# Half of the next v joined between a step's choice of experts and its counts; halves of the sums of squares added before the reduction

## Chip, cores, metric

One NeuronCore of a Trainium2 chip runs the whole program in one launch. The metric is the device time of the execution in microseconds, as the median of several runs. Single stretches come from a profile of one execution, in which every instruction has its engine, its start and its duration.

## What is computed

The first half is an attention over channels, the second a mixture of experts with one expert for each token:

```
B, N, C = 4, 5056, 256          T = B*N = 20224 tokens, E = 8, F = 1024
qn = q / (norm(q, over N) + 1e-6);  kn likewise            # norms of columns
s  = kn^T @ qn / tau                                        # C x C per batch
a  = softmax(s);   x = v @ a                                # N x C per batch
logits = x @ w_gate + modality_bias[modality_id]
e  = argmax(logits);  gate = softmax(logits)[e]
out[token] = gate * (relu(x @ w1[e]) @ w2[e])
```

All inputs are f32. The kernel splits each f32 factor of a large product in a rounded high part and a low remainder and adds three products (high by high, high by low, low by high).

## The kernel before, in words

The tokens of a batch come in NS = 10 steps of 512 (the last has 448), 40 steps g in all. Three kinds of work run beside each other.

- **q and k** (`kq_pieces`): for each step, q and k are loaded (`load`), split (`split`, lines 312 and 313), multiplied into the sum `g` in PSUM (`mm`, line 357), and squared (line 336). DVE adds the squares to `acc` (line 338), which has two halves of 2 x 256 columns, for q and for k. They are made one batch ahead.
- **softmax of a batch** (`softmax_pieces`): `norms` turns `acc` into inverse norms, by matmuls with a matrix of ones (lines 379 and 384); then `soft` per half and `gate_weights` give the attention matrix, extended by the columns of its product with w_gate.
- **a step of v** (`va_pieces`): `fetch` brings v transposed, as 16-bit halves, to the tile `T` by a transposing DMA; `part` (four DMAs in `halves`, line 506) sorts the halves into the tile `pl`; `tr(h)`, h = 0 and 1, joins them to f32 in a tile `vt` (lines 512 on ScalarE, 513 on VectorE) and splits it into `vh` and `vl` (lines 560 and 561); `av(t)`, t = 0 to 3, multiplies with the attention matrix (line 574: six matmuls into `xp`), and copies out x (lines 580, 581) and the logits `L` (line 582). `route` (lines 588 to 614) makes the one-hot choice `oh` of the experts and the running count `run` of each token's expert, and the parts of the gate. `place` (lines 625 to 647) has three small bf16 matmuls `rp`, which read `oh` and `run` and count over the partitions; from them come the rows of the tokens, and at the end `send` scatters x to its rows in the DRAM tile `xs` from GpSimd's queue. Tiles `vh` and `vl` have two buffers, `pl` and `T` one each.
- **a block of 512 rows of one expert** (`block_pieces`): from step `first_block` = 6 on one block runs per step; `load_x` and `load_w` load its rows and weights, `split_w` splits weights (lines 792, 799), `tr_x` joins and splits rows (lines 512, 513, 811, 812), `m1(j)` makes `hp` (line 826), its eviction `hh` and `hl` (lines 829, 830), and `m2(j)` the sum `y` (line 847). `pick` (lines 682 to 712) chooses the expert of a block.

For each step g the lists of pieces are merged by `_interleave` in proportion to their lengths: a block's list of about 25 pieces, the step's own list of v (10 pieces, preceded by the softmax's four where a batch begins), and q and k's list of five. The own list works for two steps at once: `turn` holds what is made for later steps (`tr` of g+1, `part` of g+2, `fetch` of g+3), `own` what belongs to g (`av` four times, `route`, `place`).

The merged list is a priority. A planner places the instructions on each engine at build time, from its own estimate of when each is ready, and may take a piece early when an engine would stand idle. At run time each engine goes through its instructions in the order given there, and waits on semaphores where data or a buffer isn't ready. All loads, `part` and `fetch` are issued from SyncE's queue (SP), the scatters from GpSimd's (POOL).

Of the kernel before, what the change touches and what calls it, by code (L numbers as in the profile page):

```python
# [14 lines left out]
ALU = mybir.AluOpType  # L15
# [20 lines left out]
def kernel(  # L36
# [13 lines left out]
    nc = tc.nc  # L50
    P = 128
    B, N, C = q.shape
# [7 lines left out]
    CH = C // P  # L60
# [24 lines left out]
    first_block = LAG + START  # L85
# [20 lines left out]
    ones = const.tile([P, P], F32, name="ones")  # L106
# [98 lines left out]
    turn = {}  # L205
# [166 lines left out]
    def softmax_pieces(b):  # L372
        st = {}

        def norms():
            a = acc[b]
            ns = ps2.tile([P, 512], F32, tag="aux", bufs=3, name=f"ns_{b}")
            for h in range(2):
                nc.tensor.matmul(
                    ns[:, 0:C], ones, a[:, h, 0:C], start=h == 0, stop=h == 1, skip_group_check=True  # L380
                )
            for m in range(CH):
                for h in range(2):
                    nc.tensor.matmul(
                        ns[:, C + m : C + m + 1], a[:, h, C + m * P : C + (m + 1) * P], ones[:, 0:1],
                        start=False, stop=h == 1, skip_group_check=True,
                    )
            inve = p1.tile([P, CH * C], F32, tag="at", name=f"inv_{b}")
            inv = inve[:, 0 : C + CH]
            roots = [nc.scalar.activation(inv, ns[:, 0 : C + CH], AF.Sqrt).ins]  # L390
            order(nc.scalar.activation(inve[:, C + CH : C + CH + 1], ones[:, 0:1], AF.Exp).ins, roots)
            nc.vector.tensor_scalar(inv, inv, 1e-6, None, ALU.add)
            nc.vector.reciprocal(inv, inv)
            rk = p1.tile([P, CH], F32, tag="rk", name=f"rk_{b}")
            nc.vector.tensor_scalar(rk, inv[:, C : C + CH], small["itau"], None, ALU.mult)
            st["rq"] = inv[:, 0:C]
            st["rk"] = rk
            st["ae"] = p1.tile([P, CH, DE], F32, tag="ae", name=f"ae_{b}")

        def soft(m):  # L400
            rq, rk, ae = st["rq"], st["rk"], st["ae"]
            sc = p3.tile([P, C], F32, tag="vt", name=f"sc_{b}_{m}")
            nc.vector.scalar_tensor_tensor(sc, gram[b][:, m, :], rk[:, m : m + 1], rq, ALU.mult, ALU.mult)
            mx = p1.tile([P, 1], F32, tag="smx", name=f"smx_{b}_{m}", bufs=2)
            nc.vector.tensor_reduce(mx, sc, AX.X, ALU.max, negate=True)
            sm = p1.tile([P, 1], F32, tag="ssm", name=f"ssm_{b}_{m}", bufs=2)
            nc.scalar.activation(sc, sc, AF.Exp, bias=mx, accum_out=sm)
            nc.vector.tensor_scalar(sm, sm, 1e-9, None, ALU.add)
            nc.vector.reciprocal(sm, sm)
            nc.vector.tensor_scalar(ae[:, m, 0:C], sc, sm, None, ALU.mult)  # L410

        def gate_weights():
            ae = st["ae"]
            tp = ps2.tile([P, 512], F32, tag="aux", bufs=3, name=f"atp_{b}")
            tv = tp.rearrange("p (j c) -> p j c", j=CH)
            at = p1.tile([P, CH, C], F32, tag="at", name=f"at_{b}")
            gw = ps2.tile([P, 512], F32, tag="aux", bufs=3, name=f"gw_{b}")
            ah = p1.tile([P, CH, DE], F32R, tag="ah", name=f"ah_{b}")
            al = p1.tile([P, CH, DE], F32R, tag="al", name=f"al_{b}")
            for m in range(CH):  # L420
                ms = slice(m * P, (m + 1) * P)
                for jh in range(CH):
                    nc.tensor.matmul(
                        tv[:, jh, ms], ae[:, m, jh * P : (jh + 1) * P], ident,
                        is_transpose=True, start=(jh == 0 and m == 0), stop=True, skip_group_check=True,
                    )
                nc.scalar.copy(at[:, :, ms], tv[:, :, ms])
                for jh in range(CH):
                    nc.tensor.matmul(
                        gw[:, m * E : (m + 1) * E], at[:, jh, ms], small["wg"][:, jh, :],  # L430
                        start=(m == 0 and jh == 0), stop=jh == CH - 1, skip_group_check=True,
                    )
                nc.scalar.copy(ah[:, m, 0:C], ae[:, m, 0:C])
                part = nc.vector.tensor_tensor(
                    al[:, m, 0:C], ae[:, m, 0:C], ah[:, m, 0:C].bitcast(F32), ALU.subtract
                ).ins
            if b == 0:
                weighted.append(("dve", part))
            gv = gw[:, 0 : CH * E].rearrange("p (m e) -> p m e", m=CH)
            ins = nc.scalar.copy(ah[:, :, C:DE], gv).ins  # L440
            softened[:] = [
                ("act", ins),
                ("dve", nc.vector.tensor_tensor(al[:, :, C:DE], gv, ah[:, :, C:DE].bitcast(F32), ALU.subtract).ins),
            ]
            attn[b] = (ah, al)

        yield norms
        for m in range(CH):
            yield lambda m=m: soft(m)
        yield gate_weights  # L450
# [4 lines left out]
    def order(ins, others):  # L455

        for other in others:
            tc.add_manual_dep(
                ins, other.name,
                mybir.DependencyInfo(mybir.DependencyClass.NoSync, mybir.DependencyReason.DATA),  # L460
                reason="order on a queue",
            )
# [24 lines left out]
    def slots_by(g):  # L487

        return max(0, g + 1 - START - sum(x <= g for x in SKIP))

    def lag(g):

        n = LAG
        for x in SKIP:
            n -= g >= x + n
        return n
# [408 lines left out]
    def run(pieces):  # L905
        for f in pieces:
            f()
# [19 lines left out]
    def once(blk, what):  # L927
        key = (blk["slot"], what)
        if key not in done:
            done.add(key)  # L930
            run(blk[what])
# [30 lines left out]
    for g in range(G):  # L962
        b, s = divmod(g, NS)
        streams = []
        for gg, blk in waiting:
            if gg <= g + 1 - lag(g + 1):
                once(blk, "load")
        if len(waiting) > 0 and waiting[0][0] <= g - lag(g):
            _, blk = waiting.pop(0)
            streams.append(block_stream(blk, waiting[0][1] if waiting and waiting[0][0] <= g + 1 - lag(g + 1) else None))  # L970
        soft = list(softmax_pieces(b)) if s == 0 and b > 0 else []
        own = list(va[g][1])
        if g - 1 in HELD:
            t = HELD[g - 1]
            own.insert(t + 1, lambda: va[g - 1][4]([copied[g, t]]))
        turn = []
        if g + 1 < first_block:
            turn.append(va[g + 1][2])
        turn += va[g + 1][0] if g + 1 < G else []
        if first_block <= g + 2 < G:  # L980
            turn.append(va[g + 2][3])
        if first_block <= g + 3 < G:
            turn.append(va[g + 3][2])
        streams.append(soft + turn + own)
        if b + 1 < B:
            if b == 0 and s == 1:
                streams.append(list(kq_pieces(1, 2, lambda: routed[1], squares[2])))
            else:
                streams.append([
                    f  # L990
                    for i in (PLAN[s] if b == 0 else [s])
                    for f in kq_pieces(
                        b + 1, i, (lambda: routed.get(g, routed[g - 1])) if b == 0 and g > 0 else (),
                        squares.setdefault(g + 1, []) if b == 0 and i == NS - 1 else None,
                    )
                ])
        _interleave(*streams)
        run(squares.get(g + 1, []))
        if waiting and waiting[0][0] <= g + 1 - lag(g + 1):
            once(waiting[0][1], "load")  # L1000
            once(waiting[0][1], "prep")
        if s == NS // 2 and b < B - 1:
            setup_bias(b + 1, routed[g])
        n = slots_by(g)
        while chosen < n:
            waiting.append((g, block_pieces(g, chosen, pick(g, chosen, False), False)))
            chosen += 1
# [84 lines left out]
```

## Time and profile before

| what | value |
|---|---|
| median of 3 runs | 1209.44 us (1208.95 to 1210.74) |
| profiled execution | 1203.36 us |
| its span, first to last instruction | 1201.6 us |
| granted TensorE clock, mean | 0.988 |
| TensorE matmul (PE) busy | 1170.8 us |
| VectorE (DVE) busy | 914.6 us |
| ScalarE (ACT) busy | 808.5 us |
| GpSimd (POOL) busy | 381.2 us |
| DMA | 228.40 MB, mean 190 GB/s |

PE stands for matmuls and PEld for loads of weights into TensorE. Times in rows of the trace are in microseconds from the start of the span. A row in order of time has start, duration, engine, line, operation, the tile written and the tiles read, the shape, and in brackets the idle time of the engine ahead of it with what ended it, where there was any. Ends of matmuls are modelled; their starts are recorded.

### The profile page before, as it was taken

Reading aid. Unit: us, or ns where it says so; the run is one execution under the profiler, and the core shown is the slowest. Engines: PE = TensorE matmul, PEld = TensorE weight load, DVE = VectorE, ACT = ScalarE, POOL = GpSimd, SP = SyncE. Lnnn points to the kernel's source line nnn. Section 1 sums busy time; section 2 is a strip of 40 time slices with the busy share of each in tenths; the row PEclk is TensorE's granted clock in tenths of the full one; section 3 lists DMA queues with packets and bytes.
Section 4 is the critical chain, followed back from the end, with each engine's and each line's share of the span. In section 5 each row is a group of like instructions: output and inputs, shape, how many; then the busy total and the mean of one; then the engine's idle time right before and its main releaser. Section 6 shows DMA issues by size and latency. Waiting matters only on the chain.

```text
span 1201.6 us, 23565 instructions
## 1 busy us (share of the span) xinstructions
PE 1170.8 (97%) x7780; PEld 1069.3 (89%) x7780; DVE 914.6 (76%) x2614; ACT 808.5 (67%) x1659; POOL 381.2 (32%) x345
## 2 busy tenths in 40 slices
PE   8986999999999999999999999999999999999996
PEld 7875999999999999899999999998999989999996
DVE  6787888987788887788888888878666777686552
ACT  6657587876777776687777777657666666556552
POOL 0053243233333333223333333332333323344221
PEclk9997999999999999899999999999999999999999
DMA  8889978597766666766666776556777564555420
GB/s 320 281 226 257 271 204 235 153 264 194 198 189 198 196 187 194 194 176 206 196 193 204 207 201 190 164 145 173 196 196 194 163 185 137 157 151 153 136 89 29
DMA packets 285844, 228.40 MB, mean 190 GB/s; under 512 B 185064, under 2 KB 243944, under 8 KB 285712
## 3 DMA queue, kind: packets, MB, share of 16 engines
q1 hardware_dynamic: 270032, 185.19, 56.9%
q0 software_dynamic: 15680, 41.61, 9.9%
q8 instruction: 63, 1.03, 0.4%
q14 instruction: 69, 0.57, 0.2%
HBM read 128.79 MB, written 43.43 MB: 143 GB/s over the span
## 4 chain that ended last, share of the span: by engine, by line
PE 71%; DVE 13%; issue 8%; ACT 4%; DMA 2%; POOL 2%; SPq 0%; POOLq 0%; ACTq 0%; DVEq 0%
PE hp L826 27%; PE y L847 26%; PE g L357 8%; PE xp L574 8%; DVE xl L812 3%; DVE hl L830 2%; POOL out_dram L469 1%; DVE vt L513 1%; ACT xt L512 1%; DVE acc L338 1%; DVE vl L561 1%; DVE xt L513 1%; DVE w1l L799 1%; ACT w1h L792 1%; DVE x L581 1%
## 5 line engine op out<-in xcount | busy, mean ns | idle before, releaser
L847 PE MATMUL y<-w2h,hh 128*128 128x256 f32 x1256 | 355.8, 283 | 0.0
L847 PE MATMUL y<-w2l,hh 128*128 128x256 f32 x1256 | 352.5, 281 | 0.0
L847 PE MATMUL y<-w2h,hl 128*128 128x256 f32 x1256 | 351.2, 280 | 0.1
L469 POOL DMA_INDIRECT xs<-x,pi x160 | 195.8, 1224 | 425.1 <-ACT hh L829 213.7
L469 POOL DMA_INDIRECT out_dram<-yo,gt x158 | 171.3, 1084 | 362.6 <-ACT hh L829 245.3
L830 DVE SCALAR_TENSOR_TENSOR hl<-hp,hh 128x512 fp32r<-128x512 f32 (+1 forms) x320 | 216.8, 678 | 50.9 <-ACT hh L829 48.9
L826 PE MATMUL hp<-xh,w1h 128*128 128x512 f32 (+1 forms) x640 | 251.2, 393 | 0.6 <-ACT xh L811 0.6
L826 PE MATMUL hp<-xl,w1h 128*128 128x512 f32 (+1 forms) x640 | 251.6, 393 | 0.0
L826 PE MATMUL hp<-xh,w1l 128*128 128x512 f32 (+1 forms) x640 | 249.4, 390 | 0.0
L847 PEld LDWEIGHTS y<-w2h,hh 128*128 128x128 f32 x1256 | 237.4, 189 | 8.7 <-ACT hh L829 0.2
L847 PEld LDWEIGHTS y<-w2l,hh 128*128 128x128 f32 x1256 | 237.2, 189 | 7.6
L847 PEld LDWEIGHTS y<-w2h,hl 128*128 128x128 f32 x1256 | 236.1, 188 | 0.3 <-DVE hl L830 0.3
L829 ACT ACTIVATE hh<-hp 128x512 fp32r<-128x512 f32 (+1 forms) x320 | 189.2, 591 | 62.5 <-PE hp L826 62.5
L792 ACT CAST w1h<-w1r 128x512 fp32r<-128x512 f32 x160 | 99.4, 621 | 175.2 <-PE hp L826 175.1
L799 DVE TENSOR_TENSOR w1l<-w1r,w1h 128x512 fp32r<-128x512 f32 x160 | 110.0, 688 | 123.4 <-ACT w1h L792 123.3
L826 PEld LDWEIGHTS hp<-xh,w1l 128*128 128x128 f32 x640 | 120.8, 189 | 26.2
L826 PEld LDWEIGHTS hp<-xh,w1h 128*128 128x128 f32 x640 | 120.8, 189 | 14.7 <-ACT xh L811 0.9
L826 PEld LDWEIGHTS hp<-xl,w1h 128*128 128x128 f32 x640 | 120.9, 189 | 13.2
L799 DVE TENSOR_TENSOR w2l<-w2r,w2h 128x512 fp32r<-128x512 f32 x160 | 109.7, 686 | 26.9 <-ACT w2h L792 23.9
L792 ACT CAST w2h<-w2r 128x512 fp32r<-128x512 f32 x160 | 100.6, 629 | 21.3 <-PE y L847 21.2
L580 ACT COPY x<-xp 128x256 uint16<-128x256 uint16 x160 | 59.0, 372 | 60.8 <-PE xp L574 44.1
L581 DVE COPY x<-xp 128x256 uint16<-128x256 uint16 x160 | 67.1, 420 | 38.3 <-ACT x L580 37.4
(160 smaller groups left out, 1873.0 us busy)
## 6 DMA issues: line engine op xcount, KB each, us to landing
w1r<-in_moe_w_dram SPq DMA_DIRECT2D x80, 512.0 KB
w2r<-in_moe_w_dram SPq DMA_DIRECT2D x80, 512.0 KB
q<-in_q_dram SPq DMA_DIRECT2D x35, 512.0 KB
k<-in_k_dram SPq DMA_DIRECT2D x35, 512.0 KB
pl<-T SPq DMA_DIRECT2D x120, 128.0 KB
v<-in_v_dram SPq DMA_DIRECT2D x6, 512.0 KB
xs<-x,pi POOLq DMA_INDIRECT x160, 5.8
out_dram<-yo,gt POOLq DMA_INDIRECT x158, 3.0
```

The costliest lines, as they stand in the source:

```text
L357: nc.tensor.matmul(gram[b][:, m, :], x, y, start=first and m == 0 and i == 0, stop=last and i == len(seq) - 1, skip_group_check=True,)
L469: ins = nc.gpsimd.indirect_dma_start(out=dst, out_offset=bass.IndirectOffsetOnAxis(ap=idx, axis=0), in_=rows, in_offset=None, bounds_check ...
L574: nc.tensor.matmul(xp[:, 0:DE], a[:, h, t * P : (t + 1) * P], w[:, h, :], start=i == 0, stop=i == len(seq) - 1,)
L580: st["out"] = nc.scalar.copy(planes[:, 0, :], halfwords[:, 1, :]).ins
L581: copied[g, t] = nc.vector.tensor_copy(planes[:, 1, :], halfwords[:, 0, :]).ins
L792: ins = nc.scalar.copy(hi, src).ins
L799: nc.vector.tensor_tensor(lo, src, hi.bitcast(F32), ALU.subtract)
L812: nc.vector.tensor_tensor(xl[:, h, 0:rows], vt[:, 0:rows], xh[:, h, 0:rows].bitcast(F32), ALU.subtract)
L826: nc.tensor.matmul(hp[:, 0:rows], w[:, h, fs], x[:, h, 0:rows], start=i == 0, stop=i == len(seq) - 1)
L829: relu = nc.scalar.activation(hh[:, 0:rows], hp[:, 0:rows], AF.Relu).ins
L830: low = nc.vector.scalar_tensor_tensor(hl[:, 0:rows], hp[:, 0:rows], 0.0, hh[:, 0:rows].bitcast(F32), ALU.max, ALU.subtract).ins
L847: ins = nc.tensor.matmul(y, a[:, tsl], w[:, j % 2, :], start=(j == 0 and i == 0 and t % per == 0), stop=(j == NJ - 1 and i == 2), skip_gro ...
```

## The change

Two places change. In `norms`, VectorE first adds the second half of `acc` to the first, and each sum over the partitions is then one matmul instead of two that accumulate. In the list of a step from g = 6 on, the pieces of `turn` and `own` are no longer one after the other: two `av`, then `tr(0)` of the next step, then two `av` and `route`, then `tr(1)`, `part` and `fetch`, then `place`. Steps before the sixth keep their order. `tr` at h = 0 also allocates the tiles of the next step (`room`).

```
         def norms():
             a = acc[b]
             ns = ps2.tile([P, 512], F32, tag="aux", bufs=3, name=f"ns_{b}")
-            for h in range(2):
+            nc.vector.tensor_tensor(a[:, 0, :], a[:, 0, :], a[:, 1, :], ALU.add)
+            nc.tensor.matmul(ns[:, 0:C], ones, a[:, 0, 0:C], start=True, stop=True, skip_group_check=True)
+            for m in range(CH):
                 nc.tensor.matmul(
-                    ns[:, 0:C], ones, a[:, h, 0:C], start=h == 0, stop=h == 1, skip_group_check=True
+                    ns[:, C + m : C + m + 1], a[:, 0, C + m * P : C + (m + 1) * P], ones[:, 0:1],
+                    start=False, stop=True, skip_group_check=True,
                 )
-            for m in range(CH):
-                for h in range(2):
-                    nc.tensor.matmul(
-                        ns[:, C + m : C + m + 1], a[:, h, C + m * P : C + (m + 1) * P], ones[:, 0:1],
-                        start=False, stop=h == 1, skip_group_check=True,
-                    )
...
-        streams.append(soft + turn + own)
+        if g < first_block:
+            streams.append(soft + turn + own)
+        else:
+            streams.append(soft + own[:2] + turn[:1] + own[2:5] + turn[1:] + own[5:])
```

## The prediction

> **What bounds the kernel now.** I read the page first (engines, the 40 slices), then the idle time of TensorE by releaser, then single steps in order of time.
>
> ```profile
> PE 1170.8 (97%) x7780; PEld 1069.3 (89%) x7780; DVE 914.6 (76%) x2614; ACT 808.5 (67%) x1659; POOL 381.2 (32%) x345
> PE   8986999999999999999999999999999999999996
> ```
>
> TensorE (PE) is busy for 97% of the span, and its holes lie in the first four slices and the last one. Between them stand steps of this kind (step 22, from its place to the one before; the columns are length, then PE, PEld, DVE, ACT, POOL busy):
>
> ```profile
> 575.06:603.72 28.66, 28.59 (x196) 26.21 (x196) 22.96 (x65) 20.56 (x43) 9.74 (x8) 1.00 0.67 202
> ```
>
> VectorE (DVE) has 5.7 us free and ScalarE (ACT) 8.1 us, PE 0.07 us by busy time. But ends of matmuls are modelled, so small waits show only in the distance from start to start. At the counts of step 22 (matmuls rp; names as in the code) PE's rows in order of time are
>
> ```profile
> 603.48 0.40 PE L826 MATMUL hp<-xh,w1l 128*128 128x512 f32 x1
> 603.72 0.19 PE L625 MATMUL rp<-oh,trim 128*128 128x32 bf16 x1
> 603.76 0.36 PE L847 MATMUL y<-w2h,hh 128*128 128x256 f32 x1
> 603.96 0.28 PE L847 MATMUL y<-w2l,hh 128*128 128x256 f32 x1
> 604.08 0.28 PE L847 MATMUL y<-w2h,hl 128*128 128x256 f32 x1
> 604.43 0.18 PE L626 MATMUL rp<-run,onesb 128*128 128x32 bf16 x1
> ```
>
> and in step 29, the last step of its batch,
>
> ```profile
> 803.85 0.40 PE L826 MATMUL hp<-xh,w1l 128*128 128x512 f32 x1
> 804.08 0.19 PE L625 MATMUL rp<-oh,trim 128*128 128x32 bf16 x1
> 804.12 0.18 PE L626 MATMUL rp<-run,onesb 128*128 128x32 bf16 x1
> 804.15 0.17 PE L627 MATMUL rp<-run,onesb 128*128 128x8 bf16 x1
> 804.17 0.37 PE L847 MATMUL y<-w2h,hh 128*128 128x256 f32 x1
> ```
>
> A y matmul is followed after 0.12 us (603.96 to 604.08). In step 22 the third y is followed only after 0.35 us, 0.23 too much, and the y behind the first rp costs 0.20 instead of 0.12: 0.31 us that step 29, with its three rp side by side, does not pay. What PE waits for is DVE:
>
> ```profile
> 598.96 0.16 DVE L582 TENSOR_TENSOR L<-xp,bsel 128x8 f32<-128x8 f32 x1
> ...
> 603.38 0.22 DVE L600 TENSOR_TENSOR oh<-val,vm 128x32 bf16<-128x32 f32 x1
> ...
> 604.16 0.22 DVE L611 TENSOR_TENSOR_SCAN run<-keep,oh 128x32 bf16<-128x32 bf16 x1
> ```
>
> The logits of the fourth piece are there at 599.1, the choice (oh) only at 603.6 and the running counts (run) at 604.38, 0.05 us before the waiting rp: 5 us for some eight small operations, because w2l, hl, acc and both joins vt with their remainders vl stand between them on DVE. In batch 3 the first rp waits too:
>
> ```profile
> 884.96 0.28 PE L847 MATMUL y<-w2l,hh 128*128 128x256 f32 x1
> 885.33 0.19 PE L625 MATMUL rp<-oh,trim 128*128 128x32 bf16 x1
> 885.37 0.36 PE L847 MATMUL y<-w2h,hl 128*128 128x256 f32 x1
> ```
>
> Here 0.37 instead of 0.12, with the extra 0.08 again: 0.33 us.
>
> **The change, part by part.** *Order of a step from g=6 on.* Slots of the step's second list before: tr(0), tr(1), part, fetch, four av, route, place; after: av, av, tr(0), av, av, route, tr(1), part, fetch, place. Place stays in slot 10, route goes from 9 to 6. No instruction is added or removed. PE follows the code's list (between two rp its rows are exactly the code's pieces), so the four av pieces, 24 matmuls, move earlier by four, four, three and three slots of about 2.9 us (28.66/10), and route with them by about 8.6 us. Even if its 5 us on DVE stay as stretched as now, run is then written some 8 us before place. That takes the waits: 0.31 us in 15 steps (11 to 17, 21 to 28), 0.33 us in 7 (31 to 37). The first and last of the 15 look alike (0.24 and 0.25 us behind their hp at 280.17 and 775.17):
>
> ```profile
> 280.41 0.19 PE L625 MATMUL rp<-oh,trim 128*128 128x32 bf16 x1
> 775.42 0.19 PE L625 MATMUL rp<-oh,trim 128*128 128x32 bf16 x1
> ```
>
> 15 x 0.31 + 7 x 0.33 = 4.7 + 2.3 = 7.0 us. Steps 6, 7, 8, 10, 20 and 30 have irregular waits of the same size; for these I take half, 6 x 0.16 = 1.0 us. Bounds of this term: 0 (the waits return elsewhere) and 8.9 us (all of the six).
>
> What covers the moved work: a join with its split is one ACT copy, one ACT cast, one DVE copy and one DVE subtract, and both halves stood in the crowded end of the step (vt, vl between lm and run). Spread over the step they use DVE's 5.7 free us; nothing on PE waits for them before av(0) of the next step, four slots after tr(1). If that cover is gone, av would wait, at most what the join is late.
>
> *Queues.* part is four SP issues, fetch one; both move from slots 3 and 4 to 8 and 9, behind the loads of q and k and those of weights that the other lists issue. SP waits at them already:
>
> ```profile
> SPq L528 <- DMA pl<-T: 61.1, 44, 3.4
> ...
> SPq L506 <- DVE vt L513: 17.1, 29, 1.9
> ```
>
> fetch waits for part's landing, part for the join. Behind them on SP stand w1r, w2r, Tx, gt, q and k; these are hidden now except once. In step 18:
>
> ```profile
> 483.49 0.21 PE L625 MATMUL rp<-oh,trim 128*128 128x32 bf16 x1 [2.58 <-DVE sm L614]
> ```
>
> ```profile
> 475.29 0.63 ACT L336 ACTIVATE acc<-k 128x512 f32<-128x512 f32 x1 [4.51 <-DMA k<-in_k_dram]
> ```
>
> ```profile
> 463.40 4.44 DMA xs<-x,pi
> ...
> 470.52 4.75 DMA k<-in_k_dram
> ```
>
> A chain of landings (xs, then k) holds ACT for 4.51 us, DVE behind it, PE 2.58 us. I leave this wait in (0): its cause, k's load behind xs on SP, is not what is moved; bounds are -2.6 (gone) and more of its kind (a rival below). POOL's scatters follow place, which stays: 0.
>
> *Norms.* Before, 8 matmul records against ones per batch for the columns (L379 x4, L384 x8); after, half of each, and one DVE add of 128x512 ahead of them. Batch 0:
>
> ```profile
> 41.74 0.86 PE ns L379 x4
> 42.60 0.80 PE ns L384 x8
> ```
>
> ```profile
> 41.07 0.69 DVE L338 TENSOR_TENSOR acc<-acc,sq_k 128x512 f32<-128x512 f32 x1 [0.60 <-ACT sq_k L336]
> ```
>
> The last add ends at 41.76, as ns begins: this is on the path. One more add of 0.69 against half of 1.66 = 0.83: -0.1, taken as 0. In batches 1 to 3, PE is the bound, and 0.83 us each goes if the add is ready in time. At batch 1 it would not be:
>
> ```profile
> 222.81 1.09 PE L379 MATMUL ns<-acc,ones 128*128 128x256 f32 x4
> 223.74 0.95 PE L384 MATMUL ns<-ones,acc 128*128 128x1 f32 x8
> 224.55 0.36 PE L847 MATMUL y<-w2h,hh 128*128 128x256 f32 x1
> ```
>
> ```profile
> 222.57 0.68 DVE L338 TENSOR_TENSOR acc<-acc,sq_k 112x512 f32<-112x512 f32 x1
> ```
>
> The last add ends at 223.25, so the new one ends at about 223.9; ns from 223.9 with 0.83 ends at 224.7, 0.2 later than now (224.55). Taken: -2 x 0.83 + 0.2 = -1.5 us. Bounds: -2.5 (all three ready) and +0.6 (all three as batch 1).
>
> The Trainium skill, page "TensorE: Matmul & The Clock Gate", section "Step-by-step: what each phase is for", speaks against this part: matmuls stay in program order and only weight loads are pulled ahead. By that rule a ns matmul whose add is late holds all y and hp behind it, and were all three batches like batch 1 this part would cost 0.6 us, and the sum would be -7.4 (estimate). The trace agrees on the order (in step 32 the y at 885.37 starts behind the late rp); whether the adds of batches 2 and 3 are late no row of before can show.
>
> **Sum.** -7.0 - 1.0 - 1.5 + 0 = -9.5 us. The profiled execution took 1203.36 us (span 1201.6 and 1.8 around it); it becomes 1193.9. The median of the runs shown, 1209.44, lies 0.5% above it; with the same difference it becomes 1199.9.
>
> **Rivals.**
> 1. *Late landings (slower).* The order on ACT, DVE and SP is fixed ahead; a load that lands later than planned stops all behind it, as k does in step 18. With part and fetch issued late in the step, q, k and weights change places with them on SP. For: step 18, 2.58 us; SP's 61.1 us at fetch. Against: one such PE wait in 34 steps. It decides from four steps on (4 x 2.58 = 10.3 > 9.5); with six, 15.5 - 9.5 = +6.0: 1215.4.
> 2. *The order hardly changes.* ACT and DVE already run joins when they can: vt of the next step sits between lm and run although its slot comes first in the list. If the joins fall back beside route, only the norms are left: -1.5, 1207.9. Against: route follows av on PE, and av moves for certain.
> 3. *More goes than I take.* Step 18's wait goes with the new order, all six irregular steps and all norms: -7.0 - 1.9 - 2.6 - 2.5 = -14.0, 1195.4.
>
> **How the numbers follow.** Forecast 0.57, rival 1 0.21, rival 2 0.14, rival 3 0.08. The forecast's own range goes from rival 3's 1195.4 to 1206.0 (the rp terms halved, norms at +0.6: -4.0 + 0.6 = -3.4). For eight in ten it must reach into rival 1: from 1193.5 (rival 3, less the 1.8 by which the runs of before differ, 1208.95 to 1210.74) to 1215. No change means within 0.2%, 2.4 us, about what a measurement of this kernel can tell. Faster: forecast, rival 3 and a little of rival 2, 0.67; same: most of rival 2, 0.12; slower: rival 1, 0.21.
>
> **What would show it.** Right: the three rp matmuls side by side in every step, about 0.23 us behind an hp or 0.12 behind a y; a step of batches 1 and 2 at 28.35 instead of 28.66 us; vt joins apart from each other on DVE; L379 x8 and L384 x16 in all. Wrong: idle time of ACT behind DMA k, q or pl in several steps, or of SP at L506 grown from 17.1 us; PE waiting at xp for vl; ns waiting for acc in all batches; or oh still within 0.3 us of its rp.

## The result and the profile after

The changed kernel took 1191.91 us (1190.73 to 1193.12, 4 runs) against 1209.58 us (1208.95 to 1210.74): ratio 0.9854, 95% interval 0.9838 to 0.987, so 17.7 us faster. The forecast of "faster" held; its size did not: 9.5 us were forecast, and the time lies 1.6 us below the range. The profiled execution has a span of 1189.0 us against 1201.6.

First the engines and the slices of the page of the changed kernel:

```profile
PE 1158.2 (97%) x7756; PEld 1059.1 (89%) x7756; DVE 924.2 (78%) x2618; ACT 807.2 (68%) x1659; POOL 373.5 (31%) x345
PE   8987999999999999999999999999999999999996
```

The shape is the same, 12.6 us shorter. PE has 24 matmul records less, DVE four instructions more (the new adds). Step 22, from rp to rp:

```profile
567.85:596.21 28.36, 28.36 (x196) 26.10 (x196) 23.27 (x65) 20.53 (x43) 9.14 (x8) 1.00 0.73 205
```

28.36 us where there were 28.66, and PE is busy for all of it. PE's rows at the counts of step 22, in order of time:

```profile
595.97 0.40 PE L823 MATMUL hp<-xh,w1l 128*128 128x512 f32 x1
596.21 0.19 PE L622 MATMUL rp<-oh,trim 128*128 128x32 bf16 x1
596.25 0.18 PE L623 MATMUL rp<-run,onesb 128*128 128x32 bf16 x1
596.28 0.17 PE L624 MATMUL rp<-run,onesb 128*128 128x8 bf16 x1
596.30 0.36 PE L844 MATMUL y<-w2h,hh 128*128 128x256 f32 x1
```

The three stand side by side, as step 29 had them before. The choice on DVE that feeds them (lines are three lower than before):

```profile
581.75 0.16 DVE L579 TENSOR_TENSOR L<-xp,bsel 128x8 f32<-128x8 f32 x1
...
584.03 0.22 DVE L597 TENSOR_TENSOR oh<-val,vm 128x32 bf16<-128x32 f32 x1
...
584.29 0.23 DVE L608 TENSOR_TENSOR_SCAN run<-keep,oh 128x32 bf16<-128x32 bf16 x1
```

From the end of the logits to the end of the counts it takes 2.6 us instead of 5.3, and the counts end at 584.52, 11.7 us ahead of the rp that reads them (596.25). Before it was 0.05 us. Of the 34 steps from step 6 on, 29 had a distance of 0.05 to 0.25 us before; after the change it is 5 to 14 us in all but step 6 (0.9). That is the change in one number: in 29 of 34 steps PE was tied to DVE with next to no slack.

What it is worth where nothing else disturbs can be read from pairs of rp, steps 11 and 17 (batch 1) and 31 and 35 (batch 3). Before, then after:

```profile
452.11 0.19 PE L625 MATMUL rp<-oh,trim 128*128 128x32 bf16 x1
859.51 0.19 PE L625 MATMUL rp<-oh,trim 128*128 128x32 bf16 x1
962.74 0.19 PE L625 MATMUL rp<-oh,trim 128*128 128x32 bf16 x1
```

```profile
278.45 0.19 PE L622 MATMUL rp<-oh,trim 128*128 128x32 bf16 x1
448.47 0.19 PE L622 MATMUL rp<-oh,trim 128*128 128x32 bf16 x1
848.14 0.19 PE L622 MATMUL rp<-oh,trim 128*128 128x32 bf16 x1
949.95 0.19 PE L622 MATMUL rp<-oh,trim 128*128 128x32 bf16 x1
```

452.11 - 280.41 = 171.70 against 170.02 us: 0.28 us a step. 103.23 against 101.81 us: 0.36 a step. 15 x 0.28 + 7 x 0.36 = 6.7 us; the forecast had 7.0 for the same 22 steps.

### The profile page after: what moved, and what is told of

It reads as the page before. It is cut to its first block, busy times and chain, and to the rows that moved or that the text cites. A ratio compares the mean times of both kernels' runs of the same rounds, so it can differ in the third digit from the quotient of the medians.

```text
span 1189.0 us, 23499 instructions
## 1 busy us (share of the span) xinstructions
PE 1158.2 (97%) x7756; PEld 1059.1 (89%) x7756; DVE 924.2 (78%) x2618; ACT 807.2 (68%) x1659; POOL 373.5 (31%) x345
## 4 chain that ended last, share of the span: by engine, by line
PE 85%; issue 6%; DVE 3%; ACT 2%; POOL 2%; DMA 1%; another core or an unknown queue 0%; POOLq 0%; SPq 0%; ACTq 0%; DVEq 0%
PE y L844 33%; PE hp L823 32%; PE g L357 10%; PE xp L571 9%; POOL out_dram L466 2%; DMA k<-in_k_dram 1%; DMA Tx<-xs 0%; DVE hl L827 0%; PE vtp L553 0%; DVE inv L390 0%; PE gw L426 0%; DVE acc L338 0%; ACT yo L858 0%; ACT w2h L789 0%
## 5 line engine op out<-in xcount | busy, mean ns | idle before, releaser
L466 POOL DMA_INDIRECT out_dram<-yo,gt x158 | 180.4, 1142 | 422.7 <-ACT hh L826 336.3
L466 POOL DMA_INDIRECT xs<-x,pi x160 | 179.6, 1122 | 358.7 <-DVE pr L690 176.9
L571 PE MATMUL xp<-ah,vh 128*128 128x264 f32 x320 | 93.4, 293 | 0.8 <-DVE pos L635 0.8
```

The lines of the kernel that those rows point to most:

```text
L466: ins = nc.gpsimd.indirect_dma_start(out=dst, out_offset=bass.IndirectOffsetOnAxis(ap=idx, axis=0), in_=rows, in_offset=None, bounds_check ...
L571: nc.tensor.matmul(xp[:, 0:DE], a[:, h, t * P : (t + 1) * P], w[:, h, :], start=i == 0, stop=i == len(seq) - 1,)
```

## Experiments

Ratios are to the kernel before, run on the same chip beside them. Three theories were to be told apart: that the gain is the waits at rp (and the norms) alone; that late landings of loads cost the kernel before more than its first profile shows, and the change hides them; and that the base of the sum, 1203.36 scaled to 1209.58, hides a uniformly slower chip.

**The kernel before, profiled again.** No edit.

> The unchanged kernel, profiled again on the chip of the timed runs. The profiled execution of before took 1203.36 us, its timed runs 1209.58 in the median: 6 us that my sum scaled away. Theory 'landings': before has waits for late DMA landings (step 18's k), whose number and length differ between executions; then this profile has a span about 1207 us with PE waits for late k or q of 3 to 9 us in all where the first profile had 2.6, and the steps that show none last 28.6 us as before. Rival 'uniform': the chip of the timed runs is slower throughout by 0.5%; then the steps of batches 1 and 2 last 28.8 us instead of 28.66 and no wait is longer. Third: the span is again 1201.6, and the difference lies outside the span or in the profiling. Timed against itself: 1.000 within 0.002.

Ratio 1.0005 (0.999 to 1.002). The span is 1209.8 us, 8.2 more than in the first profile of the same program. The undisturbed steps did not change: blocks 5 to 12 take 200.49 us from first m1 to first m1 against 200.44. So the chip is not slower throughout; the 8 us lie in single steps. In step 18, ACT and then PE:

```profile
476.49 0.63 ACT L336 ACTIVATE acc<-k 128x512 f32<-128x512 f32 x1 [5.60 <-DMA k<-in_k_dram]
```

```profile
484.70 0.21 PE L625 MATMUL rp<-oh,trim 128*128 128x32 bf16 x1 [3.67 <-DVE sm L614]
```

The load of k landed 1.1 us later with respect to ACT's need than in the first profile, and PE waited 1.1 us more (3.67 against 2.58).

The idle time is not the whole price. Beside it the granted TensorE clock stood at 0.50 for 6.8 us in both profiles (from 482.9 us in the first, from 483.9 in the second), and hp matmuls, which otherwise follow each other after 0.23 us, did so after 0.43. From the first profile, with the granted clock as the third value from the end of the first row:

```profile
484.00:488.00 4.00, 4.00 (x18) 3.62 (x18) 3.16 (x12) 3.31 (x8) 0.00 (x0) 0.50 0.56 147
486.51 0.63 PE L826 MATMUL hp<-xh,w1h 128*128 128x512 f32 x1
486.94 0.63 PE L826 MATMUL hp<-xl,w1h 128*128 128x512 f32 x1
```

PE worked through 6.3 of these 6.8 us at about half its pace, which is some 3 us lost on top of the 2.58.

Steps 20, 22, 30 and 34 are longer by 1.3, 0.7, 0.9 and 0.5 us, and step 36 by 3.6. In step 36 ACT waits in the middle of a block's last eviction, and the chain of waits names the landing of a scatter ahead of it:

```profile
977.17 0.84 ACT L861 ACTIVATE yo<-y,gt 128x256 f32<-128x256 f32 x2 [2.78 <-remote]
```

```profile
973.71 3.84 DMA xs<-x,pi
```

PE's own wait there is 1.84 us; the clock at 0.50 for 3.4 us behind it (from 978.8) makes most of the rest.

The theory of landings had said that such waits differ between executions; what it had not said is that they are spread over steps without loads of q and k too, and that the clock falls with them. In 55 runs of the kernel before, times lay between 1205.35 and 1213.78 us: the first profiled execution, 1203.36, was below all of them.

**New norms, old order.** The edit is the first part of the diff alone.

> The old order of the pieces with the new norms (one DVE add, half of the ns matmuls). My sum: -1.5 us, ratio 0.9988, bounds -2.5 to +0.6 us. Rival: the planner places later instructions otherwise because of it, step 18's wait among them, and the gain is 3 us or more (ratio below 0.9975) with the waits at rp still there in steps 11 to 17 (0.23 us at the second rp).

Ratio 0.9976 (0.9967 to 0.9985): 2.9 us faster, 1.8 to 4.0 by the interval, more than the 1.5 forecast. The interval takes in both the 2.5 us that the sum allowed and the rival's 3, so the timed runs do not decide between them. In its profile the second rp still waits, and step 18 has the longest wait of all: ACT 6.55 us for k, PE 4.02 us at rp and 0.33 at an hp ahead of it.

**New order, old norms.** The edit is the second part alone.

> The new order of the pieces with the old norms. If the parts add up, span about 1191 us in the profile (12.6 less 1.5 to 2), ratio about 0.987 to 0.988 in the timed runs. My sum by rows gave -8.0 for it, or -10.6 with step 18's wait gone: ratio 0.991 to 0.993. If the whole gain needs both parts, this one stays above 0.991.

Ratio 0.9877 (0.9863 to 0.9892), span 1190.7: 14.9 us by the order, 2.9 by the norms, 17.8 together against 17.7 measured. The parts add up, and the order is where the forecast was short: 8.0 us in the sum.

**Old order, first pieces of q and k of batches 2 and 3 held back.**

```
-  b + 1, i, (lambda: routed.get(g, routed[g - 1])) if b == 0 and g > 0 else (),
+  b + 1, i, (lambda: routed.get(g, routed[g - 1])) if g > 0 and (b == 0 or i == 0) else (),
```

> The kernel before, but the first pieces of q and k of batches 2 and 3 (casts, squares and adds of their step 0) are kept on ACT and DVE behind the last step's gate, so that no square of batch 3 sits on ACT in step 18 before its k has landed. Theory 'landings': step 18's PE wait of 2.58 us is gone, steps 12 to 14 of the blocks as long as their neighbours; gain 2.6 to 3.8 us in the span, and in the timed runs as much or more (ratio 0.994 to 0.998), since these runs have more of such waits. Rival 'uniform' or no such effect: within 0.1% of before, or slower since the pieces come too late at steps 10 and 20.

Ratio 0.9935 (0.9922 to 0.9948): 7.9 us faster, a little more than the range given. The square that waited in step 18 now runs after its data is there:

```profile
506.33 0.64 ACT L336 ACTIVATE acc<-q 128x512 f32<-128x512 f32 x1
506.98 0.63 ACT L336 ACTIVATE acc<-k 128x512 f32<-128x512 f32 x1
```

No wait stands in their brackets, and PE has none in steps 17 to 19. Blocks 12 to 15 take 88.73 us against 94.24 and 96.56 in the two profiles of before. Most of that is behind the wait of step 18: blocks 12 and 13 take 57.02 us against 62.37 and 63.35, 5.3 and 6.3 us less, which is about the wait and what was lost at the clock of 0.50 together. So early pieces of work for batch 3, of which q's square stood on ACT at 463.7 us instead of 506.3, cost these three blocks 5.5 to 7.8 us.

**The change, with the same pieces held back.** The edit of the run above in the changed kernel.

> The changed kernel, with the first pieces of q and k of batches 2 and 3 kept back as in the run that held them in the kernel before (there 0.9935 of before). In the changed kernel ACT still waits 4.9 us for the late k in step 18, but PE does not. Theory 'cover': the new order took the path from that wait to PE, so holding the pieces back brings nothing more: ratio to before 0.984 to 0.987, like the change itself (0.9854), span within 1.5 us of 1189.0. Rival 'two separate gains': the late landings are a cost of their own, and holding brings its 0.0065 again: ratio 0.979, span about 1181 to 1184.

Ratio 0.9826 (0.9805 to 0.9847), between the two theories. It was run again beside the change itself:

> The changed kernel again, beside the next two on one chip. Ratio to before 0.9854 within 0.0016. The running count stands 8 to 12 us ahead of the rp that reads it, so late landings should reach PE only in step 18 (1.6 us at hp in the first profile): the timed runs then lie within 2 us of the profiled one, where those of before lay 2 to 10 us above theirs.

> The change with the first pieces of q and k of batches 2 and 3 kept back, against the change on the same chip. 'Cover' alone says equal to the change within 0.1%; 'two separate gains' says 0.65% faster than the change. The first pair lay between: 0.9826 against 0.9854. If what remains is the wait of step 18 (1.8 us) and the longer step 20 (1.9 us), this is 0.2 to 0.3% faster than the change.

The change again: 1191.22 us (1189.74 to 1193.0), ratio 0.9857 (0.9836 to 0.9878); up to 3.3 us above its profiled execution, not the 2 I had said. Held back: 1188.46 us (1186.95 to 1189.17), ratio 0.9829 (0.9811 to 0.9846); no run of one lies among those of the other. So holding is worth 2.8 us (0.23%) in the new order and 7.9 in the old: the new order had taken about 5 us of that loss already, not all. The wait of ACT is still there after the change, and PE meets it at another place:

```profile
470.46 0.63 ACT L336 ACTIVATE acc<-k 128x512 f32<-128x512 f32 x1 [4.86 <-DMA k<-in_k_dram]
```

```profile
472.98 0.51 PE L823 MATMUL hp<-xh,w1h 128*128 128x512 f32 x1 [1.60 <-DVE hl L827]
```

Not the rp but an hp waits, for the eviction `hl` on DVE. The granted clock stays at 1.00 behind this wait. The wait of ACT in step 18 and what PE lost of it, in all profiles that have it:

| kernel | ACT waits for k | PE waits | difference | clock at 0.50 for | blocks 12 and 13 |
|---|---|---|---|---|---|
| before | 4.51 | 2.58 (rp) | 1.93 | 6.8 | 62.37 |
| before, second profile | 5.60 | 3.67 (rp) | 1.93 | 6.8 | 63.35 |
| new norms alone | 6.55 | 4.35 (rp, hp) | 2.20 | 3.4 | 63.21 |
| new order alone | 4.64 | 1.38 (hp) | 3.26 | 0 | 58.35 |
| changed kernel | 4.86 | 1.60 (hp) | 3.26 | 0 | 58.58 |
| changed kernel, second profile | 4.91 | 1.65 (hp) | 3.26 | 0 | 58.63 |
| av together, below | 4.72 | 1.46 (hp) | 3.26 | 0 | 58.34 |
| route last, below | 6.55 | 3.29 (hp) | 3.26 | 3.4 | 61.61 |
| from the first step on, below | 4.83 | 1.57 (hp) | 3.26 | 0 | 58.55 |

In the old order 1.9 to 2.2 us of lateness are free, in the new one 3.26. The landing is no earlier; the slack behind it is longer. And in most runs of the new order PE's wait is shorter and the clock does not fall beside it: the new order with the pieces held back takes 56.72 us for the two blocks, so step 18 costs the changed kernel 1.9 us where it cost the kernel before 5.3.

**The four av together.**

```
-  soft + own[:2] + turn[:1] + own[2:5] + turn[1:] + own[5:]
+  soft + turn[:1] + own[:5] + turn[1:] + own[5:]
```

> New norms; list of a step from the sixth on: tr(0), av x4, route, tr(1), part, fetch, place. Route and place are as far apart as in the change (slots 6 and 10), the four av stand together in slots 2 to 5. If the distance from route to place is what counts: ratio 0.984 to 0.988, rp matmuls side by side in every step, no PE wait in step 18. If the spreading of the av pieces counts too, the ratio lies at 0.990 or above, with waits at xp or hp.

Ratio 0.9853 (0.9825 to 0.988): the spreading of av is worth nothing that these runs show. Step 18 still has a PE wait of 1.46 us at hp, which I had expected to be gone.

**Route put back beside place.**

```
-  soft + own[:2] + turn[:1] + own[2:5] + turn[1:] + own[5:]
+  soft + own[:2] + turn[:1] + own[2:4] + turn[1:] + own[4:]
```

> New norms; list of a step from the sixth on: av, av, tr(0), av, av, tr(1), part, fetch, route, place. The av pieces stand as in the change, route is put back beside place (slots 9 and 10). Theory: what is needed is that the logits are there early; the planner takes route's operations when their data is ready, or not before route's turn. If it takes them early: ratio 0.984 to 0.988. If the place in the list rules, the DVE chain again ends at rp: 0.31 us per step in 15 steps and 0.33 in 7 come back (7 us), and step 18's wait of 2.6 to 4 us with them: ratio 0.992 to 0.995.

Ratio 0.9864 (0.9839 to 0.9889), so nearly the same. Step 22's counts and the rp that reads them:

```profile
590.86 0.22 DVE L608 TENSOR_TENSOR_SCAN run<-keep,oh 128x32 bf16<-128x32 bf16 x1
```

```profile
602.82 0.18 PE L623 MATMUL rp<-run,onesb 128*128 128x32 bf16 x1
```

11.7 us apart again, though route and place are neighbours in the list. The planner takes route's operations when the logits are there. What the changed kernel, the av together and this run share is that the four av stand in the first half of the step, ahead of `tr(1)`, `part` and `fetch`; that is what moved the choice forward, and no run separates the earlier av from the later `tr(1)`. The place of route, which gives the change its name, does not matter. Its profiled execution, the longest of the four (1197.16 us), has 3.3 us of wait in step 18 and a block 1 that is 4.6 us longer (2.46 us of wait at rp), with the clock at 0.50 for 3.4 us at each of the two; the others (1192.27 to 1193.84) show that such waits still come and go.

**The new order from the first step on.**

```
-  if g < first_block:
-      streams.append(soft + turn + own)
+  if g + 1 < first_block:
+      streams.append(soft + turn[:1] + own[:2] + turn[1:2] + own[2:5] + turn[2:] + own[5:])
```

> The change with the new order from the first step on (steps 0 to 4: next rows of v, av, av, tr(0), av, av, route, tr(1), place). Those steps end before the first block, where PE waits 6.0 us at the rp of step 4 and 3.0 us at that of step 3. If these waits go like the later ones, block 0 starts 2 to 6 us earlier than at 106.3 us and the ratio is 0.980 to 0.984. Rival: the start of block 0 hangs on the scatters and loads of its rows and on ACT, not on rp: within 1 us of 106.3, ratio 0.985; or later, since tr(1) of the next step comes after route and the steps there are only 4.6 to 11.6 us long: ratio 0.986 to 0.99.

Ratio 0.9858 (0.983 to 0.9886), block 0 at 106.49 us against 106.29: the time that the rival gave. The waits of PE at rp in steps 0 to 5 fell from 10 to 3 us, and one of 8.2 us at xp for vh came in their place:

```profile
PE xp L571 <- ACT vh L557: 8.2, 1, 8.2
PE rp L622 <- DVE sm L611: 2.4, 1, 2.4
```

So 7 us less of waiting at rp did not bring block 0 forward. Whether it hangs on the scatters and loads, as the rival says, this run does not show.

**Av together and first pieces held back.** Both edits in the changed kernel.

> The same with the four av pieces together (tr(0), av x4, route, tr(1), part, fetch, place). Since neither the spreading of av nor the place of route showed in the step lengths: equal to the run before it within 0.15%.

1186.24 us (1186.16 to 1187.0), ratio 0.9813 (0.9796 to 0.983): the fastest of all, 22.7 us below before and 5.0 below the change. Against the run before it 2.2 us or 0.19%, a little more than the 0.15% expected; in its profile block 0 starts 0.9 us earlier and many steps are shorter by 0.03 to 0.06 us; the reason stays open.

## Why the prediction was wrong

**Right: the waits at rp.** Their place, their cause (DVE's chain of the choice, with joins between), the way they go and their size: 6.7 us against 7.0. The queues part and fetch were moved past cost nothing that shows, though one sign of being wrong came: SP's idle time at part behind the join vt grew from 17.1 to 33.3 us. After step 6 PE lists no wait at xp for vh or vl. ACT and DVE had room, as their free time said. In the six irregular steps the distances of starts at rp show 2.0 us too much before and 0.1 after, where 1.0 was taken; whether the steps became shorter by that cannot be separated from the landings in them.

**Right in sign, small in size: the norms.** 2.9 us alone (1.8 to 4.0) and 2.8 beside the order, 1.5 forecast. The batch that was mis-sized is batch 1, taken as 0.2 us lost. PE's rows there, after the change:

```profile
223.42 0.40 PE L823 MATMUL hp<-xl,w1h 128*128 128x512 f32 x1
223.89 0.67 PE L379 MATMUL ns<-acc,ones 128*128 128x256 f32 x2
```

The add ends at 223.75, close to the 223.9 worked out, and ns starts 0.47 us behind the hp instead of 0.23, so 0.25 us is lost. But from the first ns to the matmul behind the last it now takes 0.87 us and not 1.74: 0.6 us won. (Before there were 12 such matmul records a batch, not the 8 of the prediction; now there are six.) In batches 2 and 3 the add ends 21 us ahead of ns and 0.88 us goes in each. A row of before could have shown that they are not late: the last squares were added 22 us ahead of ns there (784.95 against 807.05 in batch 3). The rows give 2.4 us in all.

The Trainium skill, page "TensorE: Matmul & The Clock Gate", section "Step-by-step: what each phase is for", says that matmuls stay in program order. The trace agrees: PE stood 0.25 us at the late ns of batch 1, and the next hp starts only behind it, at 224.76.

The lengths of steps in the two traces of the new order show less than these rows: 0.1 us lost in step 10, 0.4 won in step 20 and 0.8 in step 30. The rest of their difference is early, in blocks 0 to 2, and part of it is not the norms: block 0 took 25.88 us with the new norms, where the granted clock was 0.50 for 3.2 us of it, 26.52 without them, where it was 0.50 for 5.3 us of it, and 24.72 in the second profile of the changed kernel, where it was 1.00 throughout.

**Wrong: the landing in step 18, entered with 0.** The step read: "I leave this wait in (0): its cause, k's load behind xs on SP, is not what is moved". The cause indeed stayed (ACT waits 4.86 us after). But a late load costs what is left of it behind the slack between the engine that waits and PE, and the change lengthened that slack: 3.26 us of lateness are free instead of about 2. I priced the cause and not the path.

The price was wrong too. The prediction read 2.58 us as what the wait costs, and as the most that could go (-2.6); it cost 5.3 us (62.37 us for blocks 12 and 13 against 57.02 with the pieces held back), since the clock stood at 0.50 beside it for 6.8 us. The page of the kernel before shows this stretch as the one 8 among nines in its row of the clock, behind the first slices. After the change the wait is 1.60 us, the clock does not fall, and the cost is 1.9 us: 3.5 us less, where the sum had 0.

**Wrong: the base.** "With the same difference it becomes 1199.9" took the 6 us between the profiled execution and the median for something that the change leaves alone. The first profiles of the two kernels differ by 12.6 us, the timed medians by 17.7; the 5.1 between them are this step. The second profile of before shows what such differences can be: 8 us in single steps, of which those of steps 18 and 36 (4.7 us) are traced to landings and the lower clock beside the waits. That the timed runs, which left no trace, differ by the same is inferred. The time from block 15 to block 23 and from 25 to 33 (first m1 to first m1), in all profiles:

| kernels | blocks 15 to 23 | blocks 25 to 33 |
|---|---|---|
| before, first profile | 229.05 | 206.31 |
| before, second profile | 229.80 | 210.45 |
| new norms alone | 229.78 | 207.93 |
| old order, held back | 229.82 | 206.69 |
| changed kernel, both profiles | 226.72, 226.72 | 203.59, 203.59 |
| order alone, route last, from start | 226.72 each | 203.58 to 203.59 |
| held back in the new order, both profiles | 226.72, 226.72 | 203.59, 203.59 |
| av together, without and with holding | 226.35, 226.35 | 203.41, 203.41 |

In the old order the same steps differ by up to 4 us between executions; in the new order they agree to 0.01 us, with the same loads. There the counts stand 5 to 14 us ahead of rp, which leaves room for the lateness. It fits that timed runs of the changed kernel lie at most 3.3 us above their profiled ones, and those of before up to 10 above its first. Outside step 18 it is not shown that this room is what did it: the longest wait for a landing on ACT in these blocks of the new order is 2.19 us (from the first step on, at 855.2), without a longer step, but the old order took one of 1.95 us without loss as well (held back, at 859.9).

The account of the order's 14.9 us, then: 6.7 waits at rp in 22 steps; about 5 of the loss that holding the first pieces back removes, step 18's above all (7.9 by holding before, 2.8 after); some 3 are left for the irregular steps and the scattered waits, which no run separates.

Of the rivals, late landings were the right mechanism with the wrong sign: the change took them away instead of adding to them. The rival that more goes than I take named step 18, and still fell short by 3.5 us (1195.4), for the same base.

## What to carry to other kernels

Look for a consumer on the bounding engine that starts within 0.1 us of its producer's end in every step: it costs little in a quiet profile (0.3 us a step here), but lateness beyond a small slack (1.9 us here) passes straight through it. Read the granted clock behind a wait as well as the wait: here it doubled the price of the one in step 18. Giving such a pair a few microseconds of slack is worth the visible wait and the spread of the runs, so compare the profiled execution with the spread before scaling a sum. And work that a planner places far ahead of its need on an engine that goes in order should not be placed ahead of its load's landing.

## What was not expected of the hardware

The same program, on the same inputs, took between 1203.36 and 1213.78 us. In the two executions that left a profile, the difference of 8.2 us lies in single steps, and in two of them a wait for a landing is the cause (PE waits 2.58 against 3.67 us in step 18, not at all against 1.84 in step 36), while 200 us of steps between them agreed within 0.05 us.

A wait cost about twice its idle time (5.3 us for 2.58). In the thirteen profiles of this case, from 125 us to the start of the last block, PE has six listed waits of 1.84 to 4.02 us, and during or right behind each of them the granted clock stood at 0.50 for 3.4 or 6.8 us; it stood there at no other time in this stretch, and beside none of the waits of up to 1.65 us. Why the clock falls, and what happens between 1.65 and 1.84 us, no run here shows.

Listed idle time also understates ties without slack: from step 6 on the first profile of before lists 2.9 us of PE waits at rp, and the distances of starts show 9 us more, since a matmul's recorded end lies behind the start of the next.
